# Opening the first block of an MLP kernel with two token tiles in place of four

## The chip, the cores and the metric

The kernel runs on one core of a Trainium2 chip. The metric is the device time of one execution in microseconds (us); the runs listed are separate executions of the same program. A profile comes from one further execution, recorded by the hardware profiler; its times count from the span's start.

## The reference, cut to what matters

```python
B, S, D, F = 1, 2048, 1024, 3584        # x, w1, b1, w2, b2 in bf16
def reference(x, w1, b1, w2, b2):
    y = _layernorm(x, axis=-1)          # no gain, no offset
    h = _gelu(jnp.einsum("bsd,df->bsf", y, w1) + b1)
    return jnp.einsum("bsf,fd->bsd", h, w2) + b2
```

Each of the 2048 tokens is normalized over its 1024 features, multiplied by w1 into 3584 hidden features, passed through GELU (tanh form), and multiplied by w2 back to 1024 features.

## The kernel before, in words

**Tiling.** Tokens are worked in four blocks of 512 (`TB`), each of four tiles of 128 tokens. For a block the kernel computes the first product, 28 rows of 128 hidden features, then the second product, four token tiles by two halves of 512 output columns. One row of the first product is eight matmuls of 128 x 128 weights against 512 tokens, which accumulate over the eight slices of 128 features (`dt`) in one PSUM bank. ACT applies bias and GELU to the bank and writes the row to `hT_sb` in bf16 (line 364). One group of the second product is 28 matmuls of 512 columns (line 397), to which VectorE (DVE) adds b2 (line 408) before SyncE (SP) stores the tile.

**LayerNorm and transposing.** x comes with tokens on the partitions; the first product needs features there. DVE computes statistics (lines 253 and 260), GpSimd the power -1/2 (line 257), DVE normalizes in place (line 264). Then the tile is transposed into `yT_sb`. In block 0 TensorE does this (`pe_T`, line 327): eight transposes of 128 x 128 into PSUM, which ACT copies out in two copies of 512 columns (line 333). In the later blocks DVE does it with 16 instructions of 32 x 256 for each tile (`ops_T`, line 305).

**Block 0 before.** The first four rows (`R_WAVE`) are computed tile by tile, as a wave on 128 columns: for each of the four tiles, and each half of the eight slices (`K_GROUPS`), the four rows' matmuls, with the transposes of the next tile put between the two halves (lines 434 to 446). Each of the four rows holds a PSUM bank until its fourth tile is in, and then goes through GELU. From row 4 on, every row has 512 columns. The wave's first matmul waits for the transposed tile, for its w1 chunk, and for b1 (transposed by TensorE in line 429 and cast by ACT in line 431), because `new_unit` (line 342) gives that as a bank's first wait. Ahead of it TensorE runs matmuls on a tile of ones (`warm`, line 419) that compute nothing wanted, tied to the steps of the LayerNorm.

**Loads.** x, w1 and w2 are loaded whole, in the order of `SP_FIRST_LOADS` (line 26) on SP's queue and of `ACT_FIRST_LOADS` on ACT's. w1 comes in chunks of columns (`W1_CHUNK_COLS`, line 23): two of 256 columns, each split into two halves of the features (w0 to w3), two of 512 (w4, w5) and two of 1024 (w6, w7). A chunk of 256 columns has rows of 512 bytes in memory, one of 512 columns rows of 1 KB, one of 1024 rows of 2 KB. A matmul waits for the whole chunk that holds its weights (`w1_chunk_of`, line 127). Behind the list SP issues the remaining w1 chunks, x of block 1, four chunks of w2, b2, and x of blocks 2 and 3.

**Order of the work.** Every engine's program is an explicit list, written in order (`_Prog`, line 43) and emitted with semaphore waits (line 65). What DVE does behind block 0's LayerNorm is ordered by a small planner (lines 481 to 496): the additions of b2 are put in when their estimated time has come, and the LayerNorm and the transposes of the next block fill the rest. `T_PE_START`, `T_DVE_START`, `DMA_T0` and `DMA_BYTES_PER_US` are its estimates; they order DVE's list and nothing else.

Of the kernel before, what the change touches and what calls it, by code (L numbers as in the profile page):

```python
# [21 lines left out]
N_WARM_B = 3  # L22
W1_CHUNK_COLS = (256, 256, 512, 512, 1024, 1024)
W1_KSPLIT_CHUNKS = 2
N_W2_CHUNKS = 4
SP_FIRST_LOADS = ("x0a", "x2", "b1", "w0", "w1", "w2", "w3", "x3", "w4")
ACT_FIRST_LOADS = ("x0b", "x1a", "x1b")

T_PE_START = 8.5
T_DVE_START = 13.0  # L30
# [54 lines left out]
def bass_standalone__mixer_channel_mlp__prompt_kernel(  # L85
# [21 lines left out]
    R = max(1, min(R_WAVE, FT - 2, NB1 - 1))  # L107
    nkg = max(1, min(K_GROUPS, DT))
    KGROUPS = [(h * DT // nkg, (h + 1) * DT // nkg) for h in range(nkg)]
    assert NB1 + NB2 + 1 <= 8  # L110
# [31 lines left out]
    with ExitStack() as es:  # L142
# [22 lines left out]
        ps_1b = ps_1[:, :, :].bitcast(BF16)  # L165
# [105 lines left out]
        def ops_norm(i):  # L271
            if i == 0:
                y_ev[i] = [f"y{i}_{h}" for h in range(2)]
                return [op_norm(i, h * HC, (h + 1) * HC, f"y{i}_{h}") for h in range(2)]
            y_ev[i] = [f"y{i}"] * 2
            return [op_norm(i, 0, D, f"y{i}")]
# [17 lines left out]
        def ops_T(i):  # L294
            blk, t = divmod(i, TPB)
            waits = list(y_ev[i])
# [17 lines left out]
        last_te = [None]  # L314

        def pe_T(i):
            blk, t = divmod(i, TPB)
            evs = []
            for h, (j0, j1) in enumerate(KGROUPS):
                own = i == 0 and h == 1  # L320
                bank = ps_2b[:, 0, :] if own else ps_t[:, 0, :]
                o0 = j0 if own else 0
                waits = [y_ev[i][h], "ident"]
                if h == 0 and last_te[0] is not None:
                    waits.append(last_te[0])
                for j in range(j0, j1):
                    pe.op(lambda e, i=i, j=j, bank=bank, o0=o0: e.transpose(  # L327
                        out=bank[:, (j - o0) * P:(j - o0 + 1) * P], in_=x_sb[:, i, j * P:(j + 1) * P],
                        identity=ident[:, :]),
                        waits=waits if j == j0 else (), sig=(f"tp{i}_{h}" if j == j1 - 1 else None))  # L330
                src = bank[:, (j0 - o0) * P:(j1 - o0) * P].rearrange("p (j s) -> p j s", j=j1 - j0)
                dst = yT_sb[:, blk % 2, j0:j1, t * P:(t + 1) * P]
                act.op(lambda e, dst=dst, src=src: e.copy(out=dst, in_=src),  # L333
                       waits=[f"tp{i}_{h}" if i == 0 else f"tp{i}_{len(KGROUPS) - 1}"], sig=f"te{i}_{h}")
                evs += [f"te{i}_{h}"] * (j1 - j0)
            yT_ev[i] = evs
            last_te[0] = evs[-1]

        unit_n = [0]
        unit_gelu = []  # L340

        def new_unit():
            u = unit_n[0]
            unit_n[0] += 1
            return u % NB1, ([unit_gelu[u - NB1]] if u >= NB1 else ["b1c"])

        def pe_cell(b, r, t0, t1, bank, waits, sig, dts=None):
# [3 lines left out]
            for k, dt in enumerate(dts):  # L351
# [3 lines left out]
                    ps_1[:, bank, n0:n1], lhsT=w1_sb[:, dt, r * P:(r + 1) * P], rhs=yT_sb[:, b % 2, dt, n0:n1],  # L355
# [6 lines left out]
        def act_gelu(r, t0, t1, bank, wait_ev, sig):  # L362
            n0, n1 = t0 * P, t1 * P
            act.op(lambda e, r=r, n0=n0, n1=n1, bank=bank: e.activation(  # L364
                out=hT_sb[:, r, n0:n1], in_=ps_1[:, bank, n0:n1], func=ACT.Gelu_apprx_tanh,
                bias=b1_sb[:, r:r + 1], scale=1.0),
                waits=[wait_ev, "b1c"], sig=sig)
            unit_gelu.append(sig)
# [3 lines left out]
        def mm1_row(b, r):  # L372
            bank, uw = new_unit()
            sig = f"m1_{b}_{r}"
            pe_cell(b, r, 0, TPB, bank, uw, sig)
            act_gelu(r, 0, TPB, bank, sig, f"g_{b}_{r}")
            hT_row[(b, r)] = f"g_{b}_{r}"
            mm1_done[b] = sig
# [7 lines left out]
        def out_chunk(b, st, c0, c1, region, prev_store):  # L386
# [7 lines left out]
            if g >= NB2:  # L394
                waits.append(grp_oe[g - NB2])
            for ft in range(FT):
# [3 lines left out]
                    waits=(waits if ft == 0 else []) + [hT_row[(b, ft)]],  # L400
# [16 lines left out]
        def warm(n, gate=None):  # L417
            for _ in range(n):
                pe.op(lambda e: e.matmul(ps_2[:, NB2 - 1, 0:P], lhsT=ones[:, :], rhs=ones[:, :],  # L419
                                         start=True, stop=True), waits=["ones"] + ([gate] if gate else []))  # L420
# [4 lines left out]
        for o in ln_seq(list(range(TPB))):  # L425
            dve_put(o)

        pe_T(0)
        pe.op(lambda e: e.transpose(out=ps_1b[:, NB1 - 1, 0:FT], in_=b1r_sb[:, :], identity=ident[0:FT, 0:FT]),
              waits=["ident", "b1"], sig="b1t")  # L430
        act.op(lambda e: e.copy(out=b1_sb[:, :], in_=ps_1b[:, NB1 - 1, 0:FT]), waits=["b1t"], sig="b1c")  # L431
        warm(N_WARM_B)
        wave = [new_unit() for _ in range(R)]
        for t in range(TPB):
            lastt = (t == TPB - 1)
            for h, (j0, j1) in enumerate(KGROUPS):
                for r in range(R):
                    sig = f"m1_0_{r}" if lastt else f"m1_0_{r}_w{t}"
                    pe_cell(0, r, t, t + 1, wave[r][0], wave[r][1] if (t == 0 and h == 0) else [], sig,
                            dts=range(j0, j1))  # L440
                    if lastt and j1 == DT:
                        act_gelu(r, 0, TPB, wave[r][0], sig, f"g_0_{r}")
                        hT_row[(0, r)] = f"g_0_{r}"
                if t + 1 < TPB and h == 0:
# [95 lines left out]
```

## Time and profile before

| what | time |
| --- | --- |
| three runs | 399.99, 400.05 and 400.25 us, median 400.05 |
| span of the profiled execution, first to last instruction | 398.3 us |
| granted TensorE clock in it | 1.000 |
| first matmul of the first product | 7.69 us |
| first product of block 0 ends, second begins | 57.81 us |
| each later product of a block, eight groups or 28 rows | 48.35 us |
| last matmul ends | 396.46 us |

The page gives each engine's busy time, its share of the span and its count of instructions. PE is TensorE's matmuls, PEld its weight loads, which overlap them. The median of the runs is 1.75 us above the profiled span; the profiled execution's own total is not listed apart, so a change worked out on the profile is carried to the median with this distance kept. Two more parts of the page describe DMA in 40 slices of 10 us:

```profile
DMA  8999930000000000000000000000000000000001
GB/s 255 369 387 386 385 146 15 26 13 29 26 1 2 0 0 2 26 15 26 27 15 0 0 2 0 1 27 26 13 28 13 2 0 0 2 13 26 15 26 28
```

The 16 DMA engines are filled for the first 55 us, while all weights and the whole of x come in, and are almost idle afterwards.

### The profile page before, as it was taken

Reading aid. Unit: us, or ns where it says so; the run is one execution under the profiler, and the core shown is the slowest. Engines: PE = TensorE matmul, PEld = TensorE weight load, DVE = VectorE, ACT = ScalarE, POOL = GpSimd, SP = SyncE. Lnnn points to the kernel's source line nnn. Section 1 sums busy time; section 2 is a strip of 40 time slices with the busy share of each in tenths; the row PEclk is TensorE's granted clock in tenths of the full one; section 3 lists DMA queues with packets and bytes.
Section 4 is the critical chain, followed back from the end, with each engine's and each line's share of the span. In section 5 each row is a group of like instructions: output and inputs, shape, how many; then the busy total and the mean of one; then the engine's idle time right before and its main releaser. Section 6 shows DMA issues by size and latency. Waiting matters only on the chain.

```text
span 398.3 us, 4699 instructions
## 1 busy us (share of the span) xinstructions
PE 394.9 (99%) x2056; PEld 189.4 (48%) x2056; DVE 137.3 (34%) x292; ACT 82.3 (21%) x122; POOL 9.7 (2%) x25
## 2 busy tenths in 40 slices
PE   8999999999999999999999999999999999999998
PEld 7744444444444444444444444444444444444447
DVE  5207999899892004988100000001100000001011
ACT  3544430000044332000024334100003344400000
POOL 2002000200010000000000000000000000000000
DMA  8999930000000000000000000000000000000001
GB/s 255 369 387 386 385 146 15 26 13 29 26 1 2 0 0 2 26 15 26 27 15 0 0 2 0 1 27 26 13 28 13 2 0 0 2 13 26 15 26 28
DMA packets 17614, 23.64 MB, mean 59 GB/s; under 512 B 1466, under 2 KB 10042, under 8 KB 17594
## 3 DMA queue, kind: packets, MB, share of 16 engines
q1 hardware_dynamic: 17162, 22.95, 16.6%
q10 hardware_dynamic: 432, 0.39, 0.3%
q8 instruction: 16, 0.26, 0.3%
q14 instruction: 4, 0.03, 0.0%
HBM read 19.14 MB, written 4.19 MB: 59 GB/s over the span
## 4 chain that ended last, share of the span: by engine, by line
PE 99%; ACT 0%; issue 0%; DVE 0%; POOL 0%; POOLq 0%
PE ps L354 49%; PE ps L397 49%; PE ps L419 1%; PE ps_t L327 0%; ACT yT_sb L333 0%; DVE o_sb L408 0%; POOL ones L244 0%; ACT b_sb L431 0%; POOLq L525 0%
## 5 line engine op out<-in xcount | busy, mean ns | idle before, releaser
L354 PE MATMUL ps<-yT_sb,w_sb 128*128 128x512 bf16 (+1 forms) x992 | 194.8, 358 | 0.5 <-ACT b_sb L431 0.5
L397 PE MATMUL ps<-w_sb,hT_sb 128*128 128x512 bf16 (+1 forms) x980 | 194.2, 361 | 0.0
L354 PEld LDWEIGHTS ps<-yT_sb,w_sb 128*128 128x128 bf16 x992 | 91.7, 98 | 102.4 <-ACT b_sb L431 0.7
L397 PEld LDWEIGHTS ps<-w_sb,hT_sb 128*128 128x128 bf16 x980 | 91.3, 98 | 102.6
L364 ACT ACTIVATE hT_sb<-ps,b_sb 128x512 bf16<-128x512 f32 x112 | 76.7, 688 | 257.2 <-PE ps L354 257.2
L305 DVE STREAM_TRANSPOSE yT_sb<-x_sb 32x256 bf16<-32x256 bf16 x192 | 83.7, 436 | 35.0 <-PE ps L354 32.1
L408 DVE TENSOR_TENSOR o_sb<-ps,b_sb 128x512 bf16<-128x512 f32 (+1 forms) x35 | 22.6, 645 | 197.9 <-PE ps L397 197.8
L253 DVE BATCH_NORM_STATS2 st_sb<-x_sb 128x6 f32<-128x512 bf16 x32 | 21.1, 671 | 21.4 <-DMA x_sb<-in_x_dram 21.2
L257 POOL TENSOR_TENSOR rstd_sb<-mv_sb,nhalf 128x1 f32<-128x1 f32 x16 | 8.8, 551 | 111.5 <-DVE mv_sb L260 111.5
L264 DVE TENSOR_SCALAR x_sb<-x_sb,mv_sb,rstd_sb 128x1024 bf16<-128x1024 bf16 (+1 forms) x17 | 8.9, 528 | 3.7 <-POOL rstd_sb L257 2.7
L419 PE MATMUL ps<-ones 128*128 128x128 bf16 x51 | 5.4, 290 | 1.0 <-POOL ones L244 1.0
L419 PEld LDWEIGHTS ps<-ones 128*128 128x128 bf16 x51 | 4.6, 135 | 1.5 <-POOL ones L244 1.0
L333 ACT COPY yT_sb<-ps_t 128x512 bf16<-128x512 bf16 x7 | 3.8, 589 | 7.0 <-PE ps_t L327 7.0
L260 DVE BATCH_NORM_AGGREGATE mv_sb<-st_sb 128x2 f32<-128x15 f32 x16 | 3.6, 222 | 1.5
L327 PE MATMUL ps_t<-ident,x_sb 128*128 128x128 bf16 x28 | 2.2, 220 | 0.0
L422 ACT ACT_TABLE_LOAD x1 | 1.3, 1283 | 2.2 <-issue 2.2
L327 PEld LDWEIGHTS ps_t<-ident,x_sb 128*128 128x128 bf16 x28 | 1.7, 98 | 0.1
L333 ACT COPY yT_sb<-ps 128x512 bf16<-128x512 bf16 x1 | 0.6, 591 | 0.0
L327 PE MATMUL ps<-ident,x_sb 128*128 128x128 bf16 x4 | 0.4, 222 | 0.0
L245 POOL TENSOR_SCALAR_AFFINE_SELECT ident<-ones 128x128 bf16<-128x128 bf16 x1 | 0.3, 294 | 0.1
L327 PEld LDWEIGHTS ps<-ident,x_sb 128*128 128x128 bf16 x4 | 0.2, 98 | 0.1
L244 POOL MEMSET ones<- 128x128 bf16 x1 | 0.2, 205 | 0.3 <-POOLq L525 0.3
(10 smaller groups left out, 1.2 us busy)
## 6 DMA issues: line engine op xcount, KB each, us to landing
w_sb<-in_w_dram SPq DMA_DIRECT2D x4, 1792.0 KB, 18.5
w_sb<-in_w_dram SPq DMA_DIRECT2D x2, 2048.0 KB, 16.7
out_dram<-o_sb SPq DMA_DIRECT2D x31, 128.0 KB, 1.7
x_sb<-in_x_dram SPq DMA_DIRECT2D x3, 1024.0 KB, 14.2
w_sb<-in_w_dram SPq DMA_DIRECT2D x2, 1024.0 KB, 9.2
w_sb<-in_w_dram SPq DMA_DIRECT2D x4, 256.0 KB, 4.7
x_sb<-in_x_dram SPq DMA_DIRECT2D x2, 256.0 KB, 4.4
x_sb<-in_x_dram ACTq DMA_DIRECT2D x3, 128.0 KB, 3.7
```

The lines of the kernel that those rows point to most:

```text
L253: return (lambda e, i=i, h=h: e.bn_stats(st_sb[:, i, 6 * h:6 * (h + 1)], x_sb[:, i, h * HC:(h + 1) * HC]), [x_ev[i][h]], f"st{i}_{h}", 0.65)
L257: pool.op(lambda e, i=i: e.tensor_tensor(out=rstd_sb[:, i:i + 1], in0=mv_sb[:, i, 1:2], in1=nhalf[:, i:i + 1], op=ALU.pow), waits=[f"mv{i} ...
L260: return (lambda e, i=i: e.bn_aggr(mv_sb[:, i, :], st_sb[:, i, :]), [f"st{i}_0", f"st{i}_1", "eps"], f"mv{i}", 0.33)
L264: return (lambda e, i=i, c0=c0, c1=c1: e.tensor_scalar(out=x_sb[:, i, c0:c1], in0=x_sb[:, i, c0:c1], scalar1=mv_sb[:, i, 0:1], scalar2=rst ...
L305: res.append((lambda e, src=src, dst=dst: e.transpose(out=dst, in_=src), waits, (f"tr{i}" if lastop else None), 0.47))
L327: pe.op(lambda e, i=i, j=j, bank=bank, o0=o0: e.transpose(out=bank[:, (j - o0) * P:(j - o0 + 1) * P], in_=x_sb[:, i, j * P:(j + 1) * P], i ...
L333: act.op(lambda e, dst=dst, src=src: e.copy(out=dst, in_=src), waits=[f"tp{i}_{h}" if i == 0 else f"tp{i}_{len(KGROUPS) - 1}"], sig=f"te{i ...
L354: pe.op(lambda e, b=b, r=r, dt=dt, n0=n0, n1=n1, bank=bank: e.matmul(ps_1[:, bank, n0:n1], lhsT=w1_sb[:, dt, r * P:(r + 1) * P], rhs=yT_sb ...
L364: act.op(lambda e, r=r, n0=n0, n1=n1, bank=bank: e.activation(out=hT_sb[:, r, n0:n1], in_=ps_1[:, bank, n0:n1], func=ACT.Gelu_apprx_tanh, ...
L397: pe.op(lambda e, st=st, ft=ft, c0=c0, c1=c1, bank=bank: e.matmul(ps_2[:, bank, 0:c1 - c0], lhsT=hT_sb[:, ft, st * P:(st + 1) * P], rhs=w2 ...
L408: crit.append((est[sig], (lambda e, ob=ob, c0=c0, c1=c1, bank=bank: e.tensor_tensor(out=o_sb[:, ob, c0:c1], in0=ps_2[:, bank, 0:c1 - c0], ...
L419: pe.op(lambda e: e.matmul(ps_2[:, NB2 - 1, 0:P], lhsT=ones[:, :], rhs=ones[:, :], start=True, stop=True), waits=["ones"] + ([gate] if gat ...
```

## The change

Block 0 opens with two tiles (`T_PE_TILES`) instead of four. TensorE transposes tiles 0 and 1 only; DVE transposes tiles 2 and 3 with the same 16 instructions that later blocks use, right after each one's LayerNorm. The wave of four rows runs over tiles 0 and 1. Rows 4 to 25 are then computed on 256 columns, rows 26 and 27 (from `JOIN_ROW` on) on all 512, and last the second 256 columns of rows 0 to 25 are made up.

Tile 0 is normalized in two pieces, of 256 and 768 columns (`NORM_0`), and transposed in three groups of two, three and three slices (`GROUPS_0`), each with its own PSUM bank and its own copy on ACT; tile 1 in two groups. In the wave's first tile two rows at a time take turns slice by slice, and in the second tile rows run one after the other. The transposes of tile 1 stand ahead of the last eight matmuls of tile 0 (`T_AHEAD`). The transpose and the cast of b1 stand behind the first 16 matmuls (`B1_BEHIND`), and the first product no longer waits for them. The four matmuls on ones of `N_WARM_B` stand between the first and the second transpose group. The first seven rows use seven PSUM banks, the five of the first product and the two of the second.

w1 comes in six chunks of 256 columns, the first two split in halves (w0 to w3, then w4 to w7), and in four of 512 columns (w8 to w11). On SP's queue x2 (tile 2) moves behind w4 and x3 behind w8; b1 stands second.

```diff
 NOB = 2
 TAIL_PIECES = 4
 WARM_A = ((26, None), (8, "st0_0"), (8, "mv0"), (6, "rstd0"))
-N_WARM_B = 3
-W1_CHUNK_COLS = (256, 256, 512, 512, 1024, 1024)
+N_WARM_B = 4
+T_AHEAD = 8
+B1_BEHIND = 16
+NORM_0 = (0, 2, 8)
+GROUPS_0 = (0, 2, 5, 8)
+NORM_1 = (0, 8)
+GROUPS_1 = (0, 4, 8)
+T_PE_TILES = 2
+JOIN_ROW = 26
+W1_CHUNK_COLS = (256, 256, 256, 256, 256, 256, 512, 512, 512)
 W1_KSPLIT_CHUNKS = 2
 N_W2_CHUNKS = 4
-SP_FIRST_LOADS = ("x0a", "x2", "b1", "w0", "w1", "w2", "w3", "x3", "w4")
+SP_FIRST_LOADS = ("x0a", "b1", "w0", "w1", "w2", "w3", "w4", "x2", "w5", "w6", "w7", "w8", "x3")
 ACT_FIRST_LOADS = ("x0b", "x1a", "x1b")
 
-T_PE_START = 8.5
-T_DVE_START = 13.0
+T_PE_START = 6.9
+T_DVE_START = 29.0
 DMA_T0 = 2.1
 DMA_BYTES_PER_US = 0.34e6
 CRIT_SLACK = 0.3
...
     HC = D // 2
     assert ST % TB == 0 and D % P == 0 and F % P == 0 and D % NCH == 0
     assert HC <= 512 and DT * P * 2 <= 2048 and FT >= 4 and FT <= P
-    R = max(1, min(R_WAVE, FT - 2, NB1 - 1))
+    R = max(1, min(R_WAVE, FT - 2, NB1))
+    TIN = min(T_PE_TILES, TPB)
+    RJ = max(R, min(JOIN_ROW, FT))
     nkg = max(1, min(K_GROUPS, DT))
     KGROUPS = [(h * DT // nkg, (h + 1) * DT // nkg) for h in range(nkg)]
-    assert NB1 + NB2 + 1 <= 8
+    assert NB1 + NB2 + 1 <= 8 and NB2 == 2
+    assert all(c[-1] == DT for c in (NORM_0, GROUPS_0, NORM_1, GROUPS_1))
 
     w1_chunks = []
     c0 = 0
...
         y_ev = {}
 
         def ops_norm(i):
-            if i == 0:
-                y_ev[i] = [f"y{i}_{h}" for h in range(2)]
-                return [op_norm(i, h * HC, (h + 1) * HC, f"y{i}_{h}") for h in range(2)]
-            y_ev[i] = [f"y{i}"] * 2
-            return [op_norm(i, 0, D, f"y{i}")]
+            cuts = NORM_0 if i == 0 else NORM_1 if i < TIN else (0, DT)
+            y_ev[i] = []
+            res = []
+            for k, (j0, j1) in enumerate(zip(cuts[:-1], cuts[1:])):
+                res.append(op_norm(i, j0 * P, j1 * P, f"y{i}_{k}"))
+                y_ev[i] += [f"y{i}_{k}"] * (j1 - j0)
+            return res
 
         def ln_seq(tiles):
             seq = []
...
 
         def ops_T(i):
             blk, t = divmod(i, TPB)
-            waits = list(y_ev[i])
+            waits = [y_ev[i][-1]]
             if blk - 2 in mm1_done:
                 waits.append(mm1_done[blk - 2])
             res = []
...
             dve.op(o[0], waits=o[1], sig=o[2])
 
         pe_t = [T_PE_START]
-        last_te = [None]
-
-        def pe_T(i):
+        bank_read = {}
+        t_banks = [("t", ps_t[:, 0, :]), ("2_0", ps_2b[:, 0, :]), ("2_1", ps_2b[:, 1, :])]
+
+        def pe_T(i, groups, k):
             blk, t = divmod(i, TPB)
-            evs = []
-            for h, (j0, j1) in enumerate(KGROUPS):
-                own = i == 0 and h == 1
-                bank = ps_2b[:, 0, :] if own else ps_t[:, 0, :]
-                o0 = j0 if own else 0
-                waits = [y_ev[i][h], "ident"]
-                if h == 0 and last_te[0] is not None:
-                    waits.append(last_te[0])
-                for j in range(j0, j1):
-                    pe.op(lambda e, i=i, j=j, bank=bank, o0=o0: e.transpose(
-                        out=bank[:, (j - o0) * P:(j - o0 + 1) * P], in_=x_sb[:, i, j * P:(j + 1) * P],
-                        identity=ident[:, :]),
-                        waits=waits if j == j0 else (), sig=(f"tp{i}_{h}" if j == j1 - 1 else None))
-                src = bank[:, (j0 - o0) * P:(j1 - o0) * P].rearrange("p (j s) -> p j s", j=j1 - j0)
-                dst = yT_sb[:, blk % 2, j0:j1, t * P:(t + 1) * P]
-                act.op(lambda e, dst=dst, src=src: e.copy(out=dst, in_=src),
-                       waits=[f"tp{i}_{h}" if i == 0 else f"tp{i}_{len(KGROUPS) - 1}"], sig=f"te{i}_{h}")
-                evs += [f"te{i}_{h}"] * (j1 - j0)
-            yT_ev[i] = evs
-            last_te[0] = evs[-1]
+            j0, j1 = groups[k], groups[k + 1]
+            bname, bap = t_banks[k]
+            evs = yT_ev.setdefault(i, [None] * DT)
+            for j in range(j0, j1):
+                waits = []
+                if j == j0:
+                    waits = ["ident"] + ([bank_read[bname]] if bname in bank_read else [])
+                if j == j0 or y_ev[i][j] != y_ev[i][j - 1]:
+                    waits.append(y_ev[i][j])
+                pe.op(lambda e, i=i, j=j, o=(j - j0) * P, bap=bap: e.transpose(
+                    out=bap[:, o:o + P], in_=x_sb[:, i, j * P:(j + 1) * P], identity=ident[:, :]),
+                    waits=waits, sig=(f"tp{i}_{k}" if j == j1 - 1 else None))
+                evs[j] = f"te{i}_{k}"
+            src = bap[:, 0:(j1 - j0) * P].rearrange("p (j s) -> p j s", j=j1 - j0)
+            dst = yT_sb[:, blk % 2, j0:j1, t * P:(t + 1) * P]
+            act.op(lambda e, dst=dst, src=src: e.copy(out=dst, in_=src), waits=[f"tp{i}_{k}"], sig=f"te{i}_{k}")
+            bank_read[bname] = f"te{i}_{k}"
+            pe_t[0] += (j1 - j0) * 0.056
 
         unit_n = [0]
-        unit_gelu = []
+        bank_gelu = {}
+        first_ring = [("1", k) for k in range(NB1)] + [("2", 1), ("2", 0)]
 
         def new_unit():
             u = unit_n[0]
             unit_n[0] += 1
-            return u % NB1, ([unit_gelu[u - NB1]] if u >= NB1 else ["b1c"])
+            bank = first_ring[u] if u < len(first_ring) else ("1", (u - len(first_ring)) % NB1)
+            waits = [bank_gelu[bank]] if bank in bank_gelu else []
+            if bank[0] == "2" and not waits:
+                waits.append(bank_read[f"2_{bank[1]}"])
+            return bank, waits
+
+        def unit_bank(bank):
+            return (ps_1 if bank[0] == "1" else ps_2)[:, bank[1], :]
 
         def pe_cell(b, r, t0, t1, bank, waits, sig, dts=None):
             n0, n1 = t0 * P, t1 * P
...
         def act_gelu(r, t0, t1, bank, wait_ev, sig):
             n0, n1 = t0 * P, t1 * P
             act.op(lambda e, r=r, n0=n0, n1=n1, bank=bank: e.activation(
-                out=hT_sb[:, r, n0:n1], in_=ps_1[:, bank, n0:n1], func=ACT.Gelu_apprx_tanh,
+                out=hT_sb[:, r, n0:n1], in_=unit_bank(bank)[:, n0:n1], func=ACT.Gelu_apprx_tanh,
                 bias=b1_sb[:, r:r + 1], scale=1.0),
                 waits=[wait_ev, "b1c"], sig=sig)
-            unit_gelu.append(sig)
+            bank_gelu[bank] = sig
 
         hT_row = {}
 
-        def mm1_row(b, r):
+        def put_gelu(b, r, t0, t1, bank, sig):
+            act_gelu(r, t0, t1, bank, sig, f"g_{b}_{r}_{t0}")
+            for t in range(t0, t1):
+                hT_row[(b, r, t)] = f"g_{b}_{r}_{t0}"
+
+        def mm1_row(b, r, t0=0, t1=TPB):
             bank, uw = new_unit()
-            sig = f"m1_{b}_{r}"
-            pe_cell(b, r, 0, TPB, bank, uw, sig)
-            act_gelu(r, 0, TPB, bank, sig, f"g_{b}_{r}")
-            hT_row[(b, r)] = f"g_{b}_{r}"
+            sig = f"m1_{b}_{r}_{t0}"
+            pe_cell(b, r, t0, t1, bank, uw, sig)
+            put_gelu(b, r, t0, t1, bank, sig)
             mm1_done[b] = sig
 
         grp_n = [0]
...
             waits = [f"w2c{ci}" for ci in range(nw2c)]
             if g >= NB2:
                 waits.append(grp_oe[g - NB2])
+            else:
+                waits.append(bank_gelu[("2", bank)])
             for ft in range(FT):
                 pe.op(lambda e, st=st, ft=ft, c0=c0, c1=c1, bank=bank: e.matmul(
                     ps_2[:, bank, 0:c1 - c0], lhsT=hT_sb[:, ft, st * P:(st + 1) * P], rhs=w2_sb[:, ft, c0:c1],
                     start=(ft == 0), stop=(ft == FT - 1)),
-                    waits=(waits if ft == 0 else []) + [hT_row[(b, ft)]],
+                    waits=(waits if ft == 0 else []) + [hT_row[(b, ft, st)]],
                     sig=(sig if ft == FT - 1 else None))
             pe_t[0] += FT * _mm_us(c1 - c0)
             est[sig] = pe_t[0]
...
 
         def warm(n, gate=None):
             for _ in range(n):
-                pe.op(lambda e: e.matmul(ps_2[:, NB2 - 1, 0:P], lhsT=ones[:, :], rhs=ones[:, :],
+                pe.op(lambda e: e.matmul(ps_1[:, 0, 0:P], lhsT=ones[:, :], rhs=ones[:, :],
                                          start=True, stop=True), waits=["ones"] + ([gate] if gate else []))
 
         act.op(lambda e: e.preload_act_table(ACT.Gelu_apprx_tanh))
         for n, gate in WARM_A:
             warm(n, gate)
-        for o in ln_seq(list(range(TPB))):
+        for o in ln_seq(list(range(TIN))):
             dve_put(o)
-
-        pe_T(0)
-        pe.op(lambda e: e.transpose(out=ps_1b[:, NB1 - 1, 0:FT], in_=b1r_sb[:, :], identity=ident[0:FT, 0:FT]),
-              waits=["ident", "b1"], sig="b1t")
-        act.op(lambda e: e.copy(out=b1_sb[:, :], in_=ps_1b[:, NB1 - 1, 0:FT]), waits=["b1t"], sig="b1c")
+        for i in range(TIN, TPB):
+            for o in ln_seq([i]) + ops_T(i):
+                dve_put(o)
+
+        def pe_b1():
+            pe.op(lambda e: e.transpose(out=ps_t[:, 0, 0:FT], in_=b1r_sb[:, :], identity=ident[0:FT, 0:FT]),
+                  waits=["ident", "b1", bank_read["t"]], sig="b1t")
+            act.op(lambda e: e.copy(out=b1_sb[:, :], in_=ps_t[:, 0, 0:FT]), waits=["b1t"], sig="b1c")
+            bank_read["t"] = "b1c"
+
+        pe_T(0, GROUPS_0, 0)
         warm(N_WARM_B)
+        for k in range(1, len(GROUPS_0) - 1):
+            pe_T(0, GROUPS_0, k)
         wave = [new_unit() for _ in range(R)]
-        for t in range(TPB):
-            lastt = (t == TPB - 1)
-            for h, (j0, j1) in enumerate(KGROUPS):
-                for r in range(R):
-                    sig = f"m1_0_{r}" if lastt else f"m1_0_{r}_w{t}"
-                    pe_cell(0, r, t, t + 1, wave[r][0], wave[r][1] if (t == 0 and h == 0) else [], sig,
-                            dts=range(j0, j1))
-                    if lastt and j1 == DT:
-                        act_gelu(r, 0, TPB, wave[r][0], sig, f"g_0_{r}")
-                        hT_row[(0, r)] = f"g_0_{r}"
-                if t + 1 < TPB and h == 0:
-                    pe_T(t + 1)
-                    pe_t[0] += DT * 0.056
-
-        def mm1_rows(b, r0):
-            for r in range(r0, FT):
+        for t in range(TIN):
+            lastt = (t == TIN - 1)
+            if lastt:
+                order = [(r, dt) for r in range(R) for dt in range(DT)]
+            else:
+                order = [(r, dt) for r0 in range(0, R, 2) for j0, j1 in KGROUPS for dt in range(j0, j1)
+                         for r in range(r0, min(R, r0 + 2))]
+            for n, (r, dt) in enumerate(order):
+                if not lastt and n == len(order) - T_AHEAD:
+                    pe_T(t + 1, GROUPS_1, 0)
+                    pe_T(t + 1, GROUPS_1, 1)
+                if t == 0 and n == B1_BEHIND:
+                    pe_b1()
+                sig = f"m1_0_{r}_0" if lastt else f"m1_0_{r}_w{t}"
+                pe_cell(0, r, t, t + 1, wave[r][0], wave[r][1] if (t == 0 and dt == 0) else [], sig, dts=[dt])
+                if lastt and dt == DT - 1:
+                    put_gelu(0, r, 0, TIN, wave[r][0], sig)
+
+        for r in range(R, RJ):
+            mm1_row(0, r, 0, TIN)
+        for r in range(RJ, FT):
+            mm1_row(0, r)
+        if TIN < TPB:
+            for r in range(RJ):
+                mm1_row(0, r, TIN, TPB)
+
+        def mm1_rows(b):
+            for r in range(FT):
                 mm1_row(b, r)
 
-        mm1_rows(0, R)
         for b in range(NB):
             if b + 1 < NB:
                 tiles = list(range((b + 1) * TPB, (b + 2) * TPB))
```

## The prediction on record

> **What bounds the kernel now.** I read the page first, then the chain of waits, then windows of the first 20 us, the DMA issues one by one, and DVE's timeline.
>
> The page's engine row says that TensorE is busy all the time, and the chain (start us, duration us, what) says with what:
>
> ```profile
> PE 394.9 (99%) x2056; PEld 189.4 (48%) x2056; DVE 137.3 (34%) x292; ACT 82.3 (21%) x122; POOL 9.7 (2%) x25
> ...
> 6.47 1.07 ACT yT_sb L333 x2
> 7.54 0.10 ACT b_sb L431
> 7.64 0.05 issue
> 7.69 1.07 PE ps L354 x16
> 8.75 0.45 PE ps_t L327 x8
> 9.20 1.79 PE ps L354 x32
> ...
> 13.69 44.12 PE ps L354 x240
> 57.81 48.35 PE ps L397 x224
> ```
>
> From 7.69 to the end TensorE never waits. So time can be won only before 7.69, or as TensorE work left out (each later transpose group of a tile costs it 0.45), and any new wait is paid in full. Durations: a 512-column matmul takes 48.35/224 = 215.8 ns, a 128-column one 1.79/32 = 55.9 ns, with a weight load before each. The first product of block 0 ends at 57.81; the second product, the other blocks and the tail are the same in both kernels, so I compare that one moment.
>
> The second resource is DMA. Windows (window, length, five engines' busy us, PEclk, DMA share, GB/s):
>
> ```profile
> 6.00:8.00 2.00, 1.46 (x20) 1.03 (x19) 1.78 (x5) 1.16 (x3) 0.56 (x1) 1.00 1.19 302
> 10.00:12.00 2.00, 2.00 (x39) 1.98 (x37) 1.61 (x4) 0.82 (x3) 0.22 (x2) 1.00 1.10 351
> 18.00:20.00 2.00, 2.00 (x11) 0.92 (x10) 0.00 (x0) 0.96 (x3) 0.00 (x0) 1.00 1.06 388
> ```
>
> Saturated engines move 302 GB/s while the 256-column w1 chunks (rows of 512 bytes) load, 351 in 512-column chunks (1 KB), 388 in 1024-column ones (2 KB). Nobody waits for w1 today; the change asks for it twice as fast.
>
> **TensorE without DMA waits.** *Start.* Today tile 0 is normalized in two 512-column pieces (0.72 together, from 5.59); four transposes from 6.04 end at 6.44; two ACT copies (0.59 each) follow, then the cast of b1, which the first product also awaits (7.54 in the chain). Now the first piece has 256 columns. The normalize takes 402 ns for 512 columns and 545 for 1024, so by that line 330 for 256 (between 402 and 402-143 = 259): ready 5.92, transposes from 5.96, two of them done at 6.24 (one lasts 219, the next starts 56 later). A 28-column ACT operation takes 200, the 512-column copy 589; by the line a 256-column copy takes 384 and a 384-column copy 487. First copy 6.26 to 6.64; first matmul at **6.70**. Four matmuls, then a wait: group two transposes from 6.35, its copy runs 6.70 to 7.19, matmuls go on at 7.24; group three's copy ends 7.57 (two ACT copies overlap by 0.11), next go 7.62. Rows 0 and 1 are done at 7.95, half of rows 2 and 3 at 8.40. The b1 transpose and cast sit inside and gate nothing before the GELUs. The four fillers fall in the 0.28 between the transposes of groups one and two: free.
>
> *Tile 1* was normalized from 7.91 and stays so: 8.46. Its transposes, put ahead of the last eight matmuls, start at 8.50, meet no wait, and take 0.45; eight matmuls to 9.40; first copy 8.91 to 9.50, second to 9.98. Tile 1's matmuls start at 9.53, wait again before the fifth until 10.02, and end 28 x 55.9 later: **11.58**.
>
> *Rows.* No row here has 256 columns. The line through 128 (55.9) and 512 (215.8) gives 109.2; bounds are half a 512 (107.9) and two 128s (111.8), on 384 matmuls -0.5 and +1.0 us. I take the line, since both ends obey it. Rows 4 to 25: 22 x 8 x 109.2 = 19.22, to 30.80. Rows 26 and 27 on 512 columns: 16 x 215.8 = 3.45, to 34.25. The second halves of 26 rows: 208 x 109.2 = 22.71, to **56.97**. Against 57.81 that is **0.84 us won**: 0.45 x 2 of transposes gone, about a microsecond of earlier start, less what the copies' waits and narrower matmuls take.
>
> The Trainium skill ("TensorE: Matmul & The Clock Gate", Back-to-back issue gap) gives about 81 ns for each 128-column matmul in a stream with weight loads, and speaks against narrow matmuls. This trace shows 55.9 in such a stream. By its 81, the 64 narrow ones would take 1.6 us more; the row decides.
>
> *PSUM and ACT.* A 256-column GELU lasts at most the 688 ns of a 512-column one, under a row's 874 ns, and a bank returns five rows later: hidden.
>
> *DVE.* Tiles 2 and 3 need 16 transposes each. Price:
>
> ```profile
> 39.78 24.75 DVE L305 STREAM_TRANSPOSE yT_sb<-x_sb 32x256 bf16<-32x256 bf16 x55
> ```
>
> 0.45 each, 7.2 a tile; statistics to normalize take 2.85 (tile 3's, 9.63 to 12.93, less tile 2's normalize between). With x2 at 10.7 (below) tile 2 ends at 20.8; tile 3, with x3 at 19.7 to 21.2, at 30.9 to 31.3. Row 26 asks at 30.80 plus any earlier wait, so this hides behind the DMA wait below; without that it costs 0.1 to 0.5. Block 1's own LayerNorm and transposes, pushed back by some 2 us (its x now lands after 31 and DVE is free then), ended at 69.3 and are needed at 106: hidden. w2, whose last chunk landed at 49.5, comes some 2.3 later (narrower rows in all of w1) and is needed at 57: hidden.
>
> **The w1 supply.** Landing = issue + time to landing. These rows are one chunk each, a 512-column and then a 1024-column one:
>
> ```profile
> 5.39 1.85 SPq L182 DMA_DIRECT2D w_sb<-in_w_dram  x2
> ...
> w_sb<-in_w_dram SPq DMA_DIRECT2D x1, 1024.0 KB, 7.2
> w_sb<-in_w_dram SPq DMA_DIRECT2D x1, 1024.0 KB, 11.2
> w_sb<-in_w_dram SPq DMA_DIRECT2D x1, 2048.0 KB, 15.2
> ```
>
> Landings today: w0 to w3 at 6.2, 7.1, 8.1, 8.8 (0.88 per 256 KB); x3 9.6 (0.75); w4 12.6 (3.0 for 1 MB); w5, issued 5.86, 17.1; w6, issued 7.29, 22.5 (5.4 for 2 MB). w5 took 4.5 where w4 took 3.0. In that stretch one instruction fetch ran on the same DMA engines:
>
> ```profile
> q8 instruction: 1, 0.02, 3.5%
> ```
>
> That is 3.5% of 16 engines over 2 us = 1.1 us of one engine, and a chunk has landed only when its slowest engine has. What is behind it stays late: 2.0 MB after w5 land another 5.4 later, no catching up. So I take 1.5 us from the fetch on. The new kernel passes the same instruction count (about 152 matmuls) near 13.6.
>
> In the new order SP issues x0a, b1, w0 to w4, x2, w5 to w7, w8, x3. w3 (one w chunk in place of x2) lands at 8.1 + 0.88 - 0.75 = 8.2; w4 (512 KB in 512-byte rows) 10.0; x2 10.7; w5 12.5; w6 14.2; w7 16.0; w8 (1 MB) 19.0; x3 19.7; w9 22.7; w10 25.7; w11 28.7; from w6 on, 1.5 more with the fetch. SP's own issuing stays ahead: 0.5 us per 512 rows, against 0.88 to move them. TensorE, unhindered, wants them by
>
> w5 13.3, w6 15.1, w7 16.8, w8 18.6, w9 22.1, w10 25.6, w11 29.1.
>
> With the fetch the lateness is w6 0.6, w7 0.7, w8 1.9, **w9 2.1**, w10 1.6, w11 1.1. Waits don't add up, the largest counts: 2.1 us. Behind the waiting matmul stands the whole of TensorE's queue, and behind that ACT's GELUs; nothing else can be done meanwhile. Without the fetch it is 0.6 (w9). The floor is today's own row: the same bytes as up to w9 (6 MB) have landed at 22.5 although half travelled in 2 KB rows, which is 0.4 too late already.
>
> The Trainium skill ("DMA: Bandwidth & Descriptors", Specifications) calls 512 bytes enough for line rate. The windows show 302 against 388 GB/s. By its rule the twelve 256 KB of w0 to w7 would go at today's 2 KB rate (0.68 per 256 KB), an estimated 2.4 us sooner, and the wait would be gone, 399.2; the windows decide.
>
> **Sum.** -0.84 + 2.1 = +1.26 on the profiled span of 398.3: 399.6. The median of the runs, 400.05, lies 1.75 above the span; I keep that distance: **401.3**.
>
> **Rivals.** (1) *Small wait:* the fetch falls elsewhere or costs little, w9 is 0.6 late, 400.05 - 0.84 + 0.6 = 399.8; up to a 1.6 wait it stays within 0.2%. For it: the lateness of w5 hangs on one engine. Against: every later landing shares it. (2) *No wait, faster:* 512-byte rows run at the 351 of the 1 KB rows once they are long alone, 0.75 per 256 KB instead of 0.88, so that w4 to w7 take 1.0 less, and the fetch misses; w9 then lands at 21.7, nothing waits, 399.2. It decides as soon as w9 lands by 22.1. For it: x loads mixed with w0 to w3. Against: the same 6 MB at 22.5 today. (3) *Clock:* after a wait TensorE runs slow for a while. The first 26 fillers took 2.69 us, 103 ns each against 55.9; a stretch as long at half speed costs 1.3 more, 402.6. Against: the granted clock stays 1.00 across today's idle half microsecond. (4) *The join waits on DVE*, +0.1 to 0.5 in cases 1 and 2 alone.
>
> **Chances.** Forecast (wait of 1.7 to 2.7) 0.50; clock 0.07; small wait 0.27; no wait 0.16. A measurement can tell about 0.2%, 0.8 us, from no change: slower 0.57, same 0.27, faster 0.16. The range reaches from the no-wait case, 399.0, to the forecast with 256-column matmuls towards their upper bound, 402.1.
>
> **What would show it.** Right: first product near 6.7; idle time of TensorE ahead of L354 put down to w1 DMAs at rows 12 and 16; one 16 KB fetch at 13 to 14; 256-column matmuls 109 apart; first product of block 0 ending near 59. Wrong: rows 4 to 25 without gaps, or row 26 waiting for DVE.

## The result, and the profile after

The changed kernel takes **401.88 us** (median of 5 runs, 401.59 to 402.02) against 399.99 of the kernel before, taken beside it: ratio 1.0048, 95% interval 1.0037 to 1.0059. It is slower by about 1.9 us; the forecast was 401.3, slower by 1.26.

The lines below are of the changed kernel, where the first product is line 373, the transposes line 340, the GELU line 383, the fillers on ones line 444 and the second product line 422. First the page's engine row, then pieces of the chain of waits (start us, duration us, what), then TensorE's timeline (start, duration, line, what, count, and in brackets the idle time just before and what it is put down to).

```profile
PE 393.8 (98%) x2153; PEld 205.3 (51%) x2185; DVE 151.8 (38%) x324; ACT 87.4 (22%) x145; POOL 9.6 (2%) x25
...
11.80 9.35 DMA w_sb<-in_w_dram
21.15 0.14 issue
21.29 3.65 PE ps L373 x32
24.94 0.03 issue
24.97 8.89 PE ps L373 x80
```
```profile
7.36 1.30 PE L373 MATMUL ps<-yT_sb,w_sb 128*128 128x128 bf16 x16
...
9.61 6.34 PE L373 MATMUL ps<-yT_sb,w_sb 128*128 128x128 bf16 x72
...
16.51 3.68 PE L373 MATMUL ps<-yT_sb,w_sb 128*128 128x256 bf16 x32 [0.56 <-ACT hT_sb L383]
21.29 38.74 PE L373 MATMUL ps<-yT_sb,w_sb 128*128 128x256 bf16 x335 [1.09 <-DMA w_sb<-in_w_dram]
60.08 2.10 PE L422 MATMUL ps<-w_sb,hT_sb 128*128 128x512 bf16 x9
```

The first matmul comes at 7.36 instead of 7.69. The second product's first record stands at 60.08, where the timeline of the kernel before has it at 57.65 (its 57.81 is the end of the last matmul of the first product):

```profile
57.65 12.68 PE L397 MATMUL ps<-w_sb,hT_sb 128*128 128x512 bf16 x58
```

Some matmuls are missing from this trace. Its chain goes on in pieces of 49 matmuls, one starting 10.79 after the other, which is the time of 50:

```profile
60.08 10.74 PE ps L422 x49
70.82 0.05 issue
70.87 10.74 PE ps L422 x49
```

The last GELU of block 0's first product starts at 60.06 here and at 58.02 in the resident-weights run below, where the second product starts at 57.82, 0.20 ahead of it (line numbers are one higher there); so here it really starts near **59.87**:

```profile
60.06 0.47 ACT L383 ACTIVATE hT_sb<-ps,b_sb 128x256 bf16<-128x256 f32 x1 [0.40 <-PE ps L373]
```
```profile
58.02 0.47 ACT L384 ACTIVATE hT_sb<-ps,b_sb 128x256 bf16<-128x256 f32 x1 [0.40 <-PE ps L374]
```

A chain that was TensorE's from 7.69 on now runs through a w1 transfer: w8, issued at 11.80 and landed at 21.15, starts row 12 at 21.29. Row 8 stands still ahead of 16.51. The profile puts that wait down to ACT, since a GELU happened to end at 16.45; but the bank that row 8 needs had long been read, while w6 landed at 16.4. The resident-weights run below has the same GELUs and no wait there.

How much the waits cost is read better from the GELUs than from the bracketed idle time, because the ends of matmuls are modelled. Without a wait one GELU starts 0.87 after the other:

```profile
15.98 0.47 ACT L383 ACTIVATE hT_sb<-ps,b_sb 128x256 bf16<-128x256 f32 x1 [0.40 <-PE ps L373]
17.58 0.47 ACT L383 ACTIVATE hT_sb<-ps,b_sb 128x256 bf16<-128x256 f32 x1 [1.12 <-PE ps L373]
...
20.23 0.47 ACT L383 ACTIVATE hT_sb<-ps,b_sb 128x256 bf16<-128x256 f32 x1 [0.40 <-PE ps L373]
22.36 0.47 ACT L383 ACTIVATE hT_sb<-ps,b_sb 128x256 bf16<-128x256 f32 x1 [1.66 <-PE ps L373]
...
24.98 0.47 ACT L383 ACTIVATE hT_sb<-ps,b_sb 128x256 bf16<-128x256 f32 x1 [0.40 <-PE ps L373]
26.04 0.47 ACT L383 ACTIVATE hT_sb<-ps,b_sb 128x256 bf16<-128x256 f32 x1 [0.59 <-PE ps L373]
```

The GELUs of rows 8, 12 and 16 come 1.60, 2.13 and 1.06 behind their predecessors: 0.73 + 1.26 + 0.19 = **2.2 us** lost to w6, w8 and w9.

### The profile page after: what moved, and what is told of

Read it like the earlier page. It is cut to its first block, busy times and chain, and to the rows that moved or that the text cites. A ratio compares the mean times of both kernels' runs of the same rounds, so it can differ in the third digit from the quotient of the medians.

```text
span 400.6 us, 4987 instructions
## 1 busy us (share of the span) xinstructions
PE 393.8 (98%) x2153; PEld 205.3 (51%) x2185; DVE 151.8 (38%) x324; ACT 87.4 (22%) x145; POOL 9.6 (2%) x25
## 4 chain that ended last, share of the span: by engine, by line
PE 94%; SPq 3%; DMA 2%; issue 1%; DVE 0%
PE ps L422 48%; PE ps L373 46%; SPq L192 3%; DMA w_sb<-in_w_dram 2%; DVE o_sb L433 0%
## 5 line engine op out<-in xcount | busy, mean ns | idle before, releaser
L373 PE MATMUL ps<-yT_sb,w_sb 128*128 128x512 bf16 (+2 forms) x1123 | 195.4, 334 | 2.5 <-DMA w_sb<-in_w_dram 1.1
L373 PEld LDWEIGHTS ps<-yT_sb,w_sb 128*128 128x128 bf16 x1136 | 108.1, 98 | 88.9 <-ACT hT_sb L383 2.2
L383 ACT ACTIVATE hT_sb<-ps,b_sb 128x512 bf16<-128x512 f32 (+1 forms) x138 | 83.6, 606 | 256.6 <-PE ps L373 256.6
L317 DVE STREAM_TRANSPOSE yT_sb<-x_sb 32x256 bf16<-32x256 bf16 x224 | 97.6, 436 | 33.7 <-PE ps L373 30.3
L433 DVE TENSOR_TENSOR o_sb<-ps,b_sb 128x512 bf16<-128x512 f32 (+1 forms) x35 | 22.6, 646 | 198.4 <-PE ps L422 198.3
L274 DVE TENSOR_SCALAR x_sb<-x_sb,mv_sb,rstd_sb 128x1024 bf16<-128x1024 bf16 (+2 forms) x17 | 8.9, 529 | 4.9 <-POOL rstd_sb L267 4.0
L346 ACT COPY yT_sb<-ps_t 128x256 bf16<-128x256 bf16 (+1 forms) x2 | 1.0, 478 | 3.9 <-PE ps_t L340 3.9
L346 ACT COPY yT_sb<-ps 128x384 bf16<-128x384 bf16 (+1 forms) x3 | 1.5, 518 | 0.0
L340 PE MATMUL ps_t<-ident,x_sb 128*128 128x128 bf16 x6 | 0.7, 219 | 0.0
L340 PEld LDWEIGHTS ps_t<-ident,x_sb 128*128 128x128 bf16 x6 | 0.4, 98 | 0.0
## 6 DMA issues: line engine op xcount, KB each, us to landing
w_sb<-in_w_dram SPq DMA_DIRECT2D x4, 1792.0 KB, 17.9
```

The lines of the kernel that those rows point to most:

```text
L274: return (lambda e, i=i, c0=c0, c1=c1: e.tensor_scalar(out=x_sb[:, i, c0:c1], in0=x_sb[:, i, c0:c1], scalar1=mv_sb[:, i, 0:1], scalar2=rst ...
L317: res.append((lambda e, src=src, dst=dst: e.transpose(out=dst, in_=src), waits, (f"tr{i}" if lastop else None), 0.47))
L340: pe.op(lambda e, i=i, j=j, o=(j - j0) * P, bap=bap: e.transpose(out=bap[:, o:o + P], in_=x_sb[:, i, j * P:(j + 1) * P], identity=ident[:, ...
L373: pe.op(lambda e, b=b, r=r, dt=dt, n0=n0, n1=n1, bank=bank: e.matmul(unit_bank(bank)[:, n0:n1], lhsT=w1_sb[:, dt, r * P:(r + 1) * P], rhs= ...
L433: crit.append((est[sig], (lambda e, ob=ob, c0=c0, c1=c1, bank=bank: e.tensor_tensor(out=o_sb[:, ob, c0:c1], in0=ps_2[:, bank, 0:c1 - c0], ...
```

## The experiments

**Theory:** the loss is the wait for w1, wanted twice as fast as before. **Rivals:** the narrow matmuls and the two passes over the rows cost the time themselves; the new opening of tile 0 costs it; the new order of loads costs it. Each run was timed against the kernel before on the same chip, and ratios have 95% intervals. Times of the kernel before in these series were 399.8 to 399.9.

**x2 second on the queue again.**

```diff
-SP_FIRST_LOADS = ("x0a", "b1", "w0", "w1", "w2", "w3", "w4", "x2", "w5", ...
+SP_FIRST_LOADS = ("x0a", "x2", "b1", "w0", "w1", "w2", "w3", "w4", "w5", ...
```

> The changed kernel with one load moved: x of tile 2 stands second on SP's queue again, ahead of b1, and no longer behind w4. Supply theory (the loss is the wait for w1, and part of it is a hole in the DMA stream at 3.5 to 4.5 us, 38 to 55 GB/s, where x2 used to flow): the hole closes, w4 and all behind it land some 0.7 to 1.0 sooner, row 16 starts near 24.0 instead of 25.0, and the time is about 1.0 us under the changed kernel's 401.9, near 400.9. Rival (narrow matmuls and the split rows cost the time): no change, 401.9. Rival (x2 is needed late and moving it only delays w0 to w3): first wave waits, 402.5.

Measured: 401.03, ratio 1.0030 (1.0019 to 1.0042). DMA in the window from 3.5 to 4.5 us (the last two columns are the engines' busy share and GB/s), first the changed kernel, then this run:

```profile
3.50:4.50 1.00, 0.64 (x7) 0.38 (x6) 0.90 (x2) 0.00 (x0) 0.00 (x0) 1.00 0.39 47
```
```profile
3.50:4.50 1.00, 0.81 (x9) 0.54 (x8) 1.00 (x2) 0.00 (x0) 0.00 (x0) 1.00 1.15 357
```

The hole closes, x2 costs w0 to w3 nothing that shows (w3 lands at 9.2, against 8.6 to 9.3 in the four runs that have x2 further back), and w8 lands at 20.4 instead of 21.15. The medians fall by 0.85, the ratios by 0.7 us, a little less than the 1.0 of the supply theory; narrow matmuls would have left the time as it was. So this piece of the new order of loads did cost something; that the new loads as a whole are not the cause is shown by the run with the loads of the kernel before, below.

**Weights that are already there.** Rows 4 to 27 of block 0 read the weights of rows 0 to 3, so that its output is not the reference's.

```diff
+                rw = r % R if b == 0 else r
-                w = ... + [f"w1c{w1_chunk_of(r, dt)}"]      # and lhsT columns r*P
+                w = ... + [f"w1c{w1_chunk_of(rw, dt)}"]     # and lhsT columns rw*P
```

> The changed kernel, but every row of block 0's first product reads the weights of rows 0 to 3 (row modulo 4), which have landed, so no row from 4 on waits for w1; its output is not the reference's. All loads, matmuls, widths and their order stay. Supply theory: the waits of 0.56, 1.09 and some 0.2 us go, the first product of block 0 ends near 58.2 instead of 60.1, and the time is 400.0 to 400.4, within 0.1 percent of the kernel before. Rival (256-column matmuls, split rows): nothing changes, 401.9. With the prediction's own sum for TensorE alone, 0.84 won, less the 0.66 later start: 399.9.

Measured: 400.12, ratio 1.0012 (1.0003 to 1.0020). TensorE runs through:

```profile
7.51 1.30 PE L374 MATMUL ps<-yT_sb,w_sb 128*128 128x128 bf16 x16
...
9.76 48.22 PE L374 MATMUL ps<-yT_sb,w_sb 128*128 128x128 bf16 x440
57.82 4.48 PE L423 MATMUL ps<-w_sb,hT_sb 128*128 128x512 bf16 x20
```

With the w1 waits taken away, 1.4 us of the 1.9 are gone by the ratios, and 1.6 by the medians, each against the kernel before of its own series; every narrow matmul is still there. (Its twelve runs reach from 399.77 to 401.45.) From first matmul to the second product it is 57.82 - 7.51 = 50.31, in the changed kernel 59.87 - 7.36 = 52.51: 2.2 us less, as much as the GELUs gave.

**The same, with x2 second.** The edits of the two runs above together.

> The resident-weights kernel (rows 4 and up of block 0 read the weights of rows 0 to 3; output not the reference's) with x2 second on the queue. It shows what TensorE's part of the change is worth when neither w1 nor the new queue head is in the way. If the queue head with b1 second delays or scatters the arrival of tile 0 (the resident run spread from 399.77 to 401.45): narrower spread, first matmul near 7.0, 0.4 to 0.8 under the kernel before. If the narrow matmuls cost more than the line through 128 and 512 columns gives: 0.3 over the kernel before again.

```profile
7.29 1.30 PE L374 MATMUL ps<-yT_sb,w_sb 128*128 128x128 bf16 x16
...
57.59 4.70 PE L423 MATMUL ps<-w_sb,hT_sb 128*128 128x512 bf16 x21
```

Measured: 399.54, ratio 0.9992 (0.9983 to 1.0001); first matmul 7.29, second product 57.59, again 50.30 apart. The gain is 0.3, less than the 0.4 to 0.8 expected and not clear of zero. The second pass over the rows costs nothing unforeseen; the start, at 7.29 instead of 7.0, is what is missing.

**Wider chunks behind the first two pairs.**

```diff
-W1_CHUNK_COLS = (256, 256, 256, 256, 256, 256, 512, 512, 512)
+W1_CHUNK_COLS = (256, 256, 512, 512, 512, 512, 512, 512)
-SP_FIRST_LOADS = (... "w3", "w4", "x2", "w5", "w6", "w7", "w8", "x3")
+SP_FIRST_LOADS = (... "w3", "x2", "w4", "w5", "w6", "x3")
```

> The changed kernel with w1 behind the first two row pairs in chunks of 512 columns (rows of 1 KB) instead of 256 (512 bytes), with x2 ahead of the first of them and x3 behind the third. Supply theory: bytes land faster (0.75 against 0.88 us per 256 KB), but the first wide chunk, 1 MB, is wanted at 12.4 and lands at 13 to 14, so the wait moves forward to row 4, 1.0 to 1.6 us, and w9's place is no longer late; row 16 starts near 24.1 instead of 25.0, time 401.0 to 401.3. Rival (row length in memory doesn't matter, chunk size alone does): waits of 2 us or more at row 4 and none less later, 402 or above. Rival (narrow matmuls): 401.9.

Measured: 400.87, ratio 1.0018 (1.0009 to 1.0027), slightly better than expected, over runs from 399.93 to 401.60. The waits move forward, to rows 4 and 8 (0.72 and 0.95 of idle TensorE ahead of 12.58 and 17.20), and rows 12 and 16 wait no longer. Longer rows do bring the bytes sooner: from w3's landing, x2 and another 2 MB of w1 took 8.83 to 17.07 here, 9.31 to 18.15 in the changed kernel, 8.2 us against 8.8.

**Both load edits, and transposes earlier.** Wider chunks, x2 second, x3 behind w6, `T_AHEAD` 12 instead of 8.

> The changed kernel with both better loads: x2 second, 1 KB rows of w1 from the third chunk pair on with x3 behind the third of them, and tile 1's transposes 12 matmuls ahead. Supply theory: row 4 waits 0.3 to 0.5, row 8 about as much again, rows 12 and 16 not at all; 0.9 us of waits instead of 1.8, so 0.7 to 0.9 under the run with 1 KB rows alone (400.87): 400.0 to 400.2. Rival (the wait of 1 KB rows is for the chunk size and moving x2 doesn't help): 400.9.

Measured: 400.15, ratio 1.0008 (0.9999 to 1.0017), as expected: idle 0.27 ahead of row 4 and 0.38 ahead of row 8, nothing later. These better loads bring the two-tile version level with the kernel before, and no further.

**The loads of the kernel before.** `W1_CHUNK_COLS` and `SP_FIRST_LOADS` as there, all else changed.

> The changed order of work with the loads of the kernel before, chunks and queue order both. Supply theory: row 8 waits for the 512-column chunk that landed at 17.1 in the kernel before, row 12 for the first 1024-column chunk, 22.5 there, so it starts at 22.6 and the first product ends near 61.2: 3.4 over the kernel before, 403.4. Rival (narrow matmuls): 401.9, as the changed kernel. Rival (the new load order is what costs): near 400.

Measured: 402.81, ratio 1.0073 (1.0061 to 1.0085), 0.6 less than expected. The 2 MB chunk for rows 12 to 19 lands at 22.6, and row 12 starts on it:

```profile
22.69 38.55 PE L373 MATMUL ps<-yT_sb,w_sb 128*128 128x256 bf16 x336 [1.77 <-DMA w_sb<-in_w_dram]
61.08 1.24 PE L422 MATMUL ps<-w_sb,hT_sb 128*128 128x512 bf16 x5
```

So the new chunks repaired about 1 us of a wait that the new row order brought; they are not its cause.

**Fewer fillers, to move the instruction fetch.**

```diff
-WARM_A = ((26, None), (8, "st0_0"), (8, "mv0"), (6, "rstd0"))
-N_WARM_B = 4
+WARM_A = ((7, None), (2, "st0_0"), (2, "mv0"), (2, "rstd0"))   # 512 columns each
+N_WARM_B = 1
```

> The changed kernel with its 52 filler matmuls of 128 columns replaced by 14 of 512 columns: the same TensorE time with 38 matmuls fewer, so that TensorE reaches the instruction count of its first fetch some 4 us later, at 16 to 17 instead of 12.5. If that fetch is what makes one DMA engine late: w6 and w7 land at 15.4 and 17.1 instead of 16.4 and 18.2 and row 8 waits little or not at all; w8, behind the fetch still, stays near 21.1 and the time near 401.9. If the lateness has another cause: w6 at 16.4 and row 8 waiting 0.5 as before.

Measured: 401.64 (one run). The fetch moved less far than I expected, to 14.0. These are the instruction queue's lines and the landings, first the changed kernel (window 12.35 to 12.6; then w6, issued 7.87, and w7, issued 9.31), then this run (13.9 to 14.15; w6, issued 7.93, and w7, issued 9.43):

```profile
q8 instruction: 1, 0.02, 30.3%
...
w_sb<-in_w_dram SPq DMA_DIRECT2D x1, 512.0 KB, 8.5
w_sb<-in_w_dram SPq DMA_DIRECT2D x1, 512.0 KB, 8.8
```
```profile
q8 instruction: 1, 0.02, 30.1%
...
w_sb<-in_w_dram SPq DMA_DIRECT2D x1, 512.0 KB, 7.4
w_sb<-in_w_dram SPq DMA_DIRECT2D x1, 512.0 KB, 8.4
```

w6 now lands at 15.3 instead of 16.4, and row 8 goes on without a wait; w7, behind the fetch, lands at 17.9, and w8 at 20.9 much as before. Up to w5 the landings of the two executions agree (13.56 and 13.58), so nothing earlier in the queue explains it. The steps of the chunks' semaphores say the same: in the changed kernel fifteen of w6's sixteen had come by 15.31 and the last at 16.37, and fifteen of w8's by 20.07 and the last at 21.15. So a fetch makes one of the 16 engines late (30.3% of them for 0.25 us is 1.2 us of one): by 1.1 us in the changed kernel, 0.8 in this run, 1.4 in the resident-weights run; and what follows stays late. That a kernel without a fetch would lose some 1.1 us less of the 2.2 is an estimate from these steps; it wasn't tried.

**The opening alone.** Four tiles by TensorE, loads of the kernel before.

```diff
-T_PE_TILES = 2
-T_AHEAD = 8
+T_PE_TILES = 4
+T_AHEAD = 16
```

> One part of the change alone: tile 0 in three groups, b1 behind the first 16 matmuls, and the transposes of a tile 16 matmuls ahead of its end; but all four tiles are transposed by TensorE and go through the wave, so every row from 4 on has 512 columns, and the loads are those of the kernel before. Supply theory: w1 is never waited for; the first matmul starts near 7.0 instead of 7.69, the waits between the groups take 0.4 of that back: 0.2 to 0.3 faster than the kernel before. Rival (the opening itself is what costs, as the resident-weights run came out 0.3 over the kernel before): 0.3 to 0.8 slower.

Measured: 400.50, ratio 1.0014 (1.0005 to 1.0022): a miss. It was my edit, not the opening:

```profile
8.88 0.39 PE L340 MATMUL ps<-ident,x_sb 128*128 128x128 bf16 x4
9.81 0.17 PE L457 MATMUL ps_t<-ident,b1r_sb 28*128 28x28 bf16 x1 [0.54 <-ACT yT_sb L346]
```

At 16 ahead, tile 1's transposes come just before the transpose of b1, which needs the same PSUM bank, so TensorE waits 0.54 for ACT's copy, and another 0.34 before them for tile 1's normalize. With `T_AHEAD` 12 they change places:

> The opening alone with four tiles by TensorE, 12 instead of 16 matmuls ahead, which takes the same idle 0.7 us out. If that idle time was all that made the first try slower: 0.8 less than its 400.5, 399.6 to 399.7, within 0.1 percent of the kernel before. If the opening itself costs: 400.2 or above.

Measured: 399.87, ratio 0.9997 (0.9988 to 1.0006). The self-made waits were all of it, and the opening alone neither costs nor gains anything that can be told.

**Three tiles by TensorE, one by DVE.** Rows then ask for w1 every 1.3 us.

```diff
-T_PE_TILES = 2
-JOIN_ROW = 26
+T_PE_TILES = 3
+JOIN_ROW = 10        # old load order, wider chunks, T_AHEAD 16
```

> A version meant to keep the gain and to stay behind the w1 supply: three tiles by TensorE, the fourth by DVE, rows 4 to 9 on 384 columns, full rows from 10 on, old load order with 1 KB rows from the third pair on, transposes 16 matmuls ahead. A row asks for w1 every 1.3 us instead of 0.87. Supply theory: no wait for w1, one transpose group of 0.45 less than the kernel before and the earlier start: 0.6 us faster than it, near 399.2. Rival (any first product in two passes costs): 400.3 or above.

Measured: 400.17, ratio 1.0005 (0.9996 to 1.0014), a miss, with the same waits around tile 1's transposes in it. Without them, `T_AHEAD` 12:

> The three-tile version with its transposes 12 instead of 16 matmuls ahead, so that b1's transpose comes ahead of tile 1's and no longer waits for tile 1's copy to free its PSUM bank (0.7 us of TensorE idle in the run before). Supply theory: no wait for w1, first product of block 0 ends near 57.4 instead of 58.3, time 0.3 to 0.5 under the kernel before, near 399.4. Rival (two passes over the rows cost by themselves): 400.0 or above.

Measured: 399.71, ratio 0.9992 (0.9983 to 1.0001), less than the 0.3 to 0.5 us expected. No row from 4 on waits for w1 in the trace; the second product starts at 57.81, the first at 7.37. Last, with two fillers instead of six behind GpSimd's power:

> The three-tile version with two instead of six fillers behind GpSimd's power of tile 0. In the changed kernel these six took 106 ns each and held the first transposes until 6.53, though their 256-column piece of x was normalized by 6.22; in the kernel before the fillers ended with the normalize. If they are what kept the first product from starting at 6.7: first transpose about 2.7 us behind the landing of tile 0 instead of 3.0 to 3.1, 0.2 to 0.3 less time, 399.4 to 399.5. If the shorter filler group lets TensorE fall back to or stay at the slow rate for longer: no gain or 0.2 more, 399.7 to 399.9.

Measured: 399.51, ratio 0.9991 (0.9982 to 1.0001). In the profiles the first transpose comes at 6.23 instead of 6.54, and the first matmul at 7.07 instead of 7.37. It has the lowest median of the complete versions tried, about 0.3 us under the kernel before, though its interval still touches no change. That the two fillers gained anything is not shown by the times: the ratios of the two versions are 0.9992 and 0.9991, and of eleven executions with all six fillers six had the first transpose 0.06 behind the normalize too.

## Why the prediction was right, point by point

- **The side and its reason were right.** The wait for w1 was forecast at 2.1 us, with w8 and w9 latest; the GELUs show 2.2, growing by 0.7, 1.3 and 0.2 at w6, w8 and w9 where the forecast grows by 0.6, 1.2 and 0.2 there and 0.1 at w7. Taking it away gives 1.4 to 1.6 back in the times.
- **TensorE's own sum was right.** From the first matmul on it was forecast as 56.97 - 6.70 = 50.27; the two runs without w1 waits show 50.31 and 50.30. The 109.2 ns for 256 columns are the 0.87 us between GELUs, 0.874 / 8. By the 81 ns of the Trainium skill ("TensorE: Matmul & The Clock Gate", Back-to-back issue gap) for each 128-column matmul it would be an estimated 1.6 more; the measured sum has no room for that. Only the base was misread: the sum ends where the next matmul starts, and that was 57.65 before, not 57.81, so 0.68 and not 0.84 us were to be won.
- **The start was mis-sized; this is the term that failed.** Forecast 6.70, measured 7.36; in the other runs 6.71 to 7.83. Two things are in it. Tile 0's statistics began at 3.60 instead of the 3.23 of the profile I worked from, and they scatter from run to run (3.14 to 3.62 in the twelve others). And I had the first transposes wait for the normalize alone. The fillers, the last six of them gated on GpSimd's power, stand ahead of them. In the changed kernel and in the last run:

```profile
4.35 2.34 PE L444 MATMUL ps<-ones 128*128 128x128 bf16 x22 [0.36 <-DVE st_sb L263]
6.53 0.27 PE L340 MATMUL ps_t<-ident,x_sb 128*128 128x128 bf16 x2
```
```profile
4.29 1.84 PE L444 MATMUL ps<-ones 128*128 128x128 bf16 x18 [0.29 <-DVE st_sb L263]
6.23 0.29 PE L340 MATMUL ps_t<-ident,x_sb 128*128 128x128 bf16 x2
```

  Most of the 22 fillers stand 106 ns apart. The first piece of tile 0 was normalized by 5.89 + 0.33 = 6.22, and the fillers held the transposes to 6.53. With the longer piece of the kernel before they ended together with it (6.04). This too is a matter of the execution: with all the fillers, four other traces have the first transpose 0.4 to 0.5 behind the normalize, and six, in which most of the last fillers ran at 56 ns or the normalize came later, 0.06.
- **The landings were late, and that the wait still fits is luck.** From w3 to w5 all came 1.1 late (w3 9.3 for 8.2, w5 13.6 for 12.5), because I let w0 move up when x2 left; instead the DMA engines ran at 47 GB/s for a microsecond. (In the resident-weights run, with the same loads and 229 GB/s there, w3 landed at 8.6; in the run with fewer fillers, with 163, at 9.3 again.) Behind the fetch, which cost less than I took, it was 0.7 (w6 16.4 for 15.7, w8 21.15 for 20.5). As TensorE was 0.66 late too, the wait came out nearly as forecast, and the second product started 0.8 later: 59.87 for 59.07.
- **The carry to the median hid part of it.** The profiled spans differ by 2.3 where 1.26 was forecast, but the result is only 0.6 over 401.3. I kept 1.75 us between span and median. The profiled execution of the changed kernel took 401.81 for a span of 400.6, and the listed runs of the kernel before also lie about 1.2 over their spans; so the profile I worked from, 398.3, was that of an execution of some 399.5, a fast one.
- **The fetch** was forecast at 13.6 and came at about 12.5; its price was taken as 1.5 and is 1.1 here.
- **The transposes by DVE were hidden** as forecast: tile 3's end at 24.78 + 7.18 = 31.96, and row 26 begins at about 33.7. TensorE did not slow down after its waits: the GELUs behind them keep 0.87.

## What to carry to other kernels

Work that is narrowed so as to start sooner reads its weights faster; write down when each chunk lands and when the new order wants it, from the landings in the profile, before counting any engine time saved. An order of loads can be better for one consumer and leave the DMA engines idle for all, so look at GB/s in windows of half a microsecond around the edit. And when one piece of a chain is shortened, look for what else ends just behind it in the same queue: here, in five executions of eleven, fillers took 0.2 to 0.4 us of the gain. A trace is one execution; before its start times go into a sum, see how far they scatter.

## What the runs showed of the hardware

- **A hole between two loads.** In all four runs with b1 second and x2 sent back, the DMA engines moved 47 to 229 GB/s from 3.5 to 4.5 us; in the nine with x2 second and in the kernel before, 303 to 369. w0, issued at 1.7 in the four, landed at 5.8 to 6.6, hardly sooner than behind x2 (6.0 to 7.0). Why its packets start so late is open.
- **A late DMA engine stays late.** One 16 KB fetch held up one of the 16 engines, so that chunks landed 0.8 to 1.4 us late, and the lateness was not made up. The Trainium skill ("Runtime: NRT & Kernel Launch", Instruction fetch mechanics) has instructions fetched in blocks of 16 KiB, at a cost that is mostly hidden. The blocks agree; TensorE's rows show no stop when the fetch ran at 12.5, but where DMA bounds the stage its cost came back as 0.7 us ahead of row 8.
- **The slow rate of the first matmuls.** Fillers ran at 103 to 106 ns where later 128-column matmuls take 56, in one execution until past 6.5 us. The Trainium skill ("TensorE: Matmul & The Clock Gate", What's actually happening) tells of half rate until the array has been busy for a free-running window of some 3.4 us, so that the moment varies from run to run. That fits; the granted clock in the profile, 1.00 throughout, does not show it.
